# Reordered weight loads and a first token block in two halves, in a sketched-attention and squared-ReLU FFN kernel on one Trainium2 core

## Chip, cores and metric

The kernel runs on one NeuronCore of a Trainium2 chip. The metric is device time in microseconds (us), the median of several runs; lower is better. All else is read from one profiled execution of the kernel.

## What is computed

Polynomial-sketch linear attention over 4 batches, 4 heads, 1088 tokens and head size 32 is followed by a feed-forward block (FFN) with squared ReLU, from d_model 128 to d_ff 2048 and back. Everything is float32.

```python
def phi(x):                                   # x: [b, h, s, 32]
    a = np.einsum('rd,bhsd->bhsr', S1, x)     # r = 8
    b = np.einsum('rd,bhsd->bhsr', S2, x)
    return np.einsum('bhsi,bhsj->bhsij', a, b).reshape(*x.shape[:-1], 64)
q_p, k_p = phi(q), phi(k)
kv = np.einsum('bhsf,bhsd->bhfd', k_p, v)
z = np.sum(k_p, axis=2)
num = np.einsum('bhsf,bhfd->bhsd', q_p, kv)
den = np.einsum('bhsf,bhf->bhs', q_p, z)[..., None] + 1e-06
x = (num / den).transpose(0, 2, 1, 3).reshape(4352, 128)
h = np.maximum(x @ w_in, 0.0)
return h * h @ w_out
```

## The kernel before

The attention result is kept transposed in `xT` (128 features by 4352 tokens). The FFN walks over ten token chunks (`FC`: 256, 384, 448, 448, then five of 512 and a last one of 256). For a chunk, d_ff is cut into 16 blocks of 128. A *unit* is a group of blocks that fills one PSUM tile of 512 columns: in the first chunk two units of one block and seven of two blocks. Each unit goes through four steps:

- `ffn1` (L600): first matmul, `pg <- xT, w_in`, in the one-pass type fp32r. One record of the trace per block.
- `relu` (L610 on VectorE, L612 on ScalarE): `gt <- pg`.
- `square` (L623 on ScalarE, L625 on VectorE): `g <- gt`.
- `ffn2` (L644; L639 for the last chunk): second matmul, `po <- g, w_o`, in fp32, summed over the 16 blocks in PSUM. Two records per block.

`pg` has two PSUM buffers, so the first matmul of a unit waits for the relu two units back.

The first 256 tokens of batch 0 have a path of their own, written out by hand before line 854: `kf` (L318) sketches the keys with weights 64 or 32 columns wide, `kvp` (L399) sums keys against values, and `dT`, `rd`, `bc` and `xT` (L847 to L854, all on VectorE) form the reciprocal of the denominator, spread it and multiply. Between them `a_rep_kv` (L449, ScalarE) copies kv, and one matmul on `w_in` (L845, tile `warm`) is issued before the first FFN matmul. The rest of batch 0 comes in two further chunks of 384 and 448 tokens. Each takes these steps: transpose of q (`qT`, L299, VectorE), sketch of q (`qc`, L306, TensorE), reciprocals of the denominators (`rc`, L505), 16 small copies of them on GpSimd (`rd`, L513), shuffles and products (L522, L537), numerators (`nd`, L553, TensorE), the spread of the reciprocals (`bc`, L563) and the product into `xT` (L570). The first 384-wide FFN matmul needs that second chunk's `xT`.

Loads are issued on SyncE's queue in the order of the program, and each waits for the one eight places earlier to land: k, q's first 256 tokens and v of batch 0, q's next 384, the pieces of `w_in` (256 KB each, L208) and `w_o` (L217), q's last 448, and then batches 1 and 2. GpSimd casts each piece of `w_in` to fp32r (L688), ahead of its `rd` copies. Piece c of either weight serves blocks 4c to 4c+3.

```python
load_wi(nc.sync, 0)
load_wi(nc.sync, 1)
load_wi(nc.sync, 2)
load_wo(nc.sync, 0)
load_wo(nc.sync, 1)
load_wi(nc.sync, 3)
for c in range(2, 4):
    load_wo(nc.sync, c)
load_q(nc.sync, 0, 640, S)
```

From there on the order of instructions on each engine comes from a planner, `_Order`: operations with estimated times, needs and keys are placed greedily, engine by engine, and then emitted. TensorE's FFN order is fixed in advance by `seq`: the first matmuls of `LU = 4` units run ahead, and then each step emits the second matmuls of one unit (two units after the first chunk) and the first matmuls of units that come due. Batch 1's loads (`loads`) are such an operation. v of batch 1 has padding columns that GpSimd sets to zero, with a memset early in the program.

`f_last` closes the kernel: the last 256 tokens lie in `po[0]` and `po[1]`, ScalarE copies the first to SBUF (L682), VectorE the second (L684), and each is stored by two DMAs.

## Time and profile before

| | us |
|---|---|
| median of 3 runs | 185.08 |
| lowest and highest | 184.76, 185.16 |
| the profiled execution: its own time | 184.68 |
| its span from first to last instruction | 182.8 |
| TensorE busy | 177.8 (97%) |
| ScalarE busy | 136.5 (75%) |
| VectorE busy | 121.8 (67%) |
| GpSimd busy | 38.5 (21%) |

PE is TensorE's matmuls, PEld its weight loads, DVE VectorE, ACT ScalarE, POOL GpSimd, SP SyncE; a q behind the name is the engine's instruction queue, which waits or issues DMAs. A row of the timeline gives the start, the length and the engine of a merged group, its line, operation, tiles (written <- read) and shapes, the number of records, and in brackets the engine's idle time just before it with what ended it. Ends of matmuls are modelled, so successive matmuls may overlap in the rows; starts are the safer reading. A slice of the page is 4.57 us, a digit the share in tenths.

### The profile page before, as it was taken

The page shows a single profiled execution, that of the slowest core. Times are in us where ns is not written, and L with a number is a line of the kernel's source. Part 1 is how long each engine was busy: PE and PEld are TensorE (multiplying, and loading weights), DVE is VectorE, ACT ScalarE, POOL GpSimd, SP SyncE. Part 2 cuts the span into 40 slices and gives each one's busy share as a digit, 9 for nine tenths or more (in the row PEclk, how much of TensorE's full clock was granted, in tenths as well). Part 3 has the DMA queues.
Part 4 walks back from the last instruction along what each step waited for, and adds up shares of the span by engine and source line. Part 5 has one row for each costly group of instructions (what it writes and reads, how often), then busy time and mean ns, then how long its engine had stood idle before and what let it go on. Part 6 is the DMA issues. An engine that isn't in the chain of part 4 may idle for free.

```text
span 182.8 us, 3998 instructions
## 1 busy us (share of the span) xinstructions
PE 177.8 (97%) x1530; PEld 104.8 (57%) x1530; DVE 121.8 (67%) x262; ACT 136.5 (75%) x259; POOL 38.5 (21%) x158
## 2 busy tenths in 40 slices
PE   8999899999999999999999999999999999999992
PEld 2868676655645655555455554545555555555792
DVE  5979679999999962799994335996353334333640
ACT  3449479849948886799937778894777777777990
POOL 3545208438300002570008100500000000000000
PEclk9999999999999999999999999999999999999999
DMA  5799994010029700000030200003003000300111
GB/s 172 194 285 305 234 251 132 4 32 0 0 39 243 181 0 4 4 2 0 0 54 14 43 0 5 0 0 59 0 4 57 0 0 5 52 0 0 33 28 29
DMA packets 26147, 11.26 MB, mean 62 GB/s; under 512 B 17937, under 2 KB 25105, under 8 KB 26129
## 3 DMA queue, kind: packets, MB, share of 16 engines
q1 hardware_dynamic: 25936, 10.95, 24.9%
q8 instruction: 12, 0.20, 0.5%
q10 hardware_dynamic: 192, 0.07, 0.1%
q14 instruction: 7, 0.05, 0.1%
HBM read 8.78 MB, written 2.23 MB: 60 GB/s over the span
## 4 chain that ended last, share of the span: by engine, by line
PE 86%; SPq 6%; DMA 4%; DVE 1%; issue 1%
PE po L644 58%; PE pg L600 17%; DMA qn<-in_q_dram 4%; PE nd L553 3%; PE po L639 2%; PE pol L639 2%; SPq L217 2%; SPq L199 2%; SPq L208 1%; PE qc L306 1%; PE nd L417 1%; PE qc L350 1%; PE kvp L417 1%; SPq L187 0%; SPq L181 0%
## 5 line engine op out<-in xcount | busy, mean ns | idle before, releaser
L644 PE MATMUL po<-g,w_o 128*128 128x512 f32 (+3 forms) x288 | 122.7, 547 | 0.1
L612 ACT ACTIVATE gt<-pg 128x512 f32<-128x512 f32 (+3 forms) x144 | 75.2, 570 | 32.1 <-PE pg L600 31.5
L644 PEld LDWEIGHTS po<-g,w_o 128*128 128x128 f32 x288 | 53.4, 189 | 32.1 <-issue 24.4
L600 PE MATMUL pg<-xT,w_in 128*128 128x512 f32 (+3 forms) x160 | 70.1, 519 | 0.5 <-DVE xT L570 0.5
L623 ACT ACTIVATE g<-gt 128x512 f32<-128x512 f32 (+2 forms) x102 | 60.7, 623 | 1.6
L625 DVE TENSOR_TENSOR g<-gt 128x512 f32<-128x512 f32 (+3 forms) x43 | 30.0, 699 | 39.5 <-ACT gt L612 38.8
L600 PEld LDWEIGHTS pg<-xT,w_in 128*128 128x128 f32 x160 | 29.2, 190 | 29.2 <-ACT gt L612 11.5
L513 POOL COPY rd<-rc 32x9 f32<-32x9 f32 (+2 forms) x80 | 19.1, 239 | 27.0 <-DVE rc L505 23.8
L459 POOL COPY kv<-kvt 32x64 f32<-32x64 f32 x48 | 12.7, 264 | 44.7 <-DVE kvt L436 42.5
L522 DVE STREAM_SHUFFLE qa<-qc 128x576 f32<-128x576 f32 (+2 forms) x20 | 11.8, 652 | 0.0
L537 DVE TENSOR_TENSOR qp<-qa,qb 128x576 f32<-128x576 f32 (+2 forms) x20 | 10.8, 605 | 0.0
L485 DVE STREAM_TRANSPOSE qt<-qc 128x576 f32<-128x576 f32 (+2 forms) x10 | 5.8, 610 | 5.7 <-PE qc L350 4.0
L370 DVE TENSOR_TENSOR kp<-fs 128x576 f32<-128x576 f32 x12 | 8.8, 747 | 0.0
L648 DVE STREAM_TRANSPOSE oT<-po 128x512 f32<-128x512 f32 (+3 forms) x9 | 5.9, 654 | 2.1 <-PE po L644 2.1
L299 DVE STREAM_TRANSPOSE qT<-qn 128x192 f32<-128x192 f32 (+3 forms) x11 | 5.8, 560 | 1.7 <-DMA qn<-in_q_dram 1.7
L553 PE MATMUL nd<-qp,kv 32*32 32x288 f32 (+2 forms) x320 | 6.6, 354 | 0.0
L522 DVE STREAM_SHUFFLE qb<-qc 128x576 f32<-128x576 f32 (+2 forms) x10 | 6.1, 650 | 0.0
L570 DVE TENSOR_TENSOR xT<-nd,bc 128x576 fp32r<-128x576 f32 (+2 forms) x10 | 5.6, 594 | 0.5 <-PE nd L553 0.5
L639 PE MATMUL po<-w_o,g 128*128 128x128 f32 x32 | 5.8, 279 | 0.0
L639 PE MATMUL pol<-w_o,g 128*128 128x128 f32 x32 | 5.7, 275 | 0.0
L563 DVE STREAM_TRANSPOSE bc<-rd 128x576 f32<-128x576 f32 (+2 forms) x10 | 5.7, 598 | 0.0
L553 PEld LDWEIGHTS nd<-qp,kv 32*32 32x32 f32 x320 | 2.9, 103 | 3.6 <-issue 2.4
(106 smaller groups left out, 90.0 us busy)
## 6 DMA issues: line engine op xcount, KB each, us to landing
kn<-in_k_dram SPq DMA_DIRECT2D x3, 544.0 KB, 8.3
qn<-in_q_dram SPq DMA_DIRECT2D x3, 544.0 KB, 9.8
vn<-in_v_dram SPq DMA_DIRECT2D x9, 144.0 KB, 6.6
w_in<-in_moe_w_in_dram SPq DMA_DIRECT2D x4, 256.0 KB, 4.3
w_o<-in_moe_w_out_dram SPq DMA_DIRECT2D x4, 256.0 KB, 5.2
out_dram<-oT SPq DMA_DIRECT2D x12, 64.0 KB, 1.9
out_dram<-oT SPq DMA_DIRECT2D x8, 56.0 KB, 1.8
out_dram<-oT SPq DMA_DIRECT2D x8, 48.0 KB, 1.8
```

Source lines behind the costliest of these rows:

```text
L370: nc.vector.tensor_tensor(out=_ap(st[b, "kp"], 0, 128, 64 * NT * h, [[64, NT], [8, 8], [1, 8]]), in0=_ap(fs, 0, 128, o, [[32, NT], [1, 8], ...
L459: nc.gpsimd.tensor_copy(_ap(st[b, "kv"], 32 * c, 32, 64 * h, [[32, E], [1, 32]]), _ap(st["kvt"], 32 * h, 32, 0, [[64, E], [1, 32]]),)
L513: nc.gpsimd.tensor_copy(st[b, "rd", i0][32 * h : 32 * h + 32, n * c : n * c + n], st["rc"][32 * c : 32 * c + 32, n * h : n * h + n],)
L522: nc.vector.stream_shuffle(in_=banks(st[b, "qc", i0], 2 * x, 0, m), out=_ap(st[b, which, i0], 0, 128, 2 * m * x, [[m, 2], [1, m]]), mask=m ...
L537: nc.vector.tensor_tensor(out=st[b, "qp", i0, e][:, r], in0=st[b, f"qa{e}", i0][:, r], in1=st[b, "qb", i0][:, r], op=mult,)
L553: nc.tensor.matmul(nd[32 * h : 32 * h + 32, 512 * c : 512 * c + m], kv[r, o : o + 32], qp[r, m * h : m * h + m], start=(e == 0), stop=(e = ...
L600: nc.tensor.matmul(st["pg", u][:, n * i : n * i + n], w_in[:, 128 * (d0 + i) : 128 * (d0 + i) + 128], xT[:, c0 : c0 + n],)
L612: nc.scalar.activation(gt[:, 0:w], st["pg", u][:, 0:w], Relu)
L623: nc.scalar.activation(to, of, Square)
L625: nc.vector.tensor_tensor(out=to, in0=of, in1=of, op=mult)
L639: nc.tensor.matmul(po[x // 128][:, 0:128], g[:, x : x + 128], w, start=(d == 0), stop=(d == NB - 1),)
L644: nc.tensor.matmul(po[0][:, 0:n], w, g, start=(d == 0), stop=(d == NB - 1))
```

## The change

- The weight pieces alternate: w_in 0, w_o 0, w_in 1, w_o 1, w_in 2, w_o 2, w_in 3, then q's last 448 tokens, then w_o 3.
- The zeros of batch 1's v are written by GpSimd behind the second chunk's `rd` copies, and the zeroed range takes in the last column of a v row. v of batch 1 (its fourth part first) and q of batch 1 are issued behind that memset. For later batches v's parts are reversed too.
- The spread `bc0` and the product into `xT` of the first 256 tokens come in two halves of 128. Between them the first matmul and the relu of block 0 for the first half are emitted, and then the copy of kv; the square of that half is emitted behind, ahead of the next transpose of q.
- Block 0 of the first chunk is now two units of 128 tokens each, followed by block 1 alone and seven units of two blocks. The relu on VectorE is now that of block 1 (unit 2).
- `LU` becomes 3 for the first two steps of `seq` and 4 behind them.
- The matmul on `w_in` at L845 goes; the two key-sketch tiles with 64-wide weights become 32-wide.
- In `f_last` the second copy is cut: VectorE copies 64 columns and ScalarE the other 64.

```diff
-    LU = 4
+    LU = 3, 4
...
-            sizes = [1, 1] + [2] * 7
+            sizes = [1] + [2] * 7
+            d0 = 1
+            units += [(0, c0, 128, 0, 1)] * 2
+            dur += [5 * 128 / 2400 + 0.015] * 2
...
-            xT[:, c0 : c0 + n],
+            xT[:, c0 + part.get(u, 0) : c0 + part.get(u, 0) + n],
...
-            nc.tensor.matmul(po[0][:, 0:n], w, g, start=(d == 0), stop=(d == NB - 1))
+            x = part.get(u, 0)
+            nc.tensor.matmul(
+                po[0][:, x : x + n], w, g, start=(d == 0 and x == 0), stop=(d == NB - 1),
+                skip_group_check=(ci == 0),
+            )
...
-        nc.vector.tensor_copy(ob[1][:, :], po[1][:, 0:128])
+        nc.vector.tensor_copy(ob[1][:, 0:64], po[1][:, 0:64])
+        nc.scalar.copy(ob[1][:, 64:128], po[1][:, 64:128])
...
-    load_wi(nc.sync, 0)
-    load_wi(nc.sync, 1)
-    load_wi(nc.sync, 2)
-    load_wo(nc.sync, 0)
-    load_wo(nc.sync, 1)
-    load_wi(nc.sync, 3)
-    for c in range(2, 4):
+    for c in range(4):
+        load_wi(nc.sync, c)
+        if c == 3:
+            load_q(nc.sync, 0, 640, S)
         load_wo(nc.sync, c)
-    load_q(nc.sync, 0, 640, S)
...
-    nc.gpsimd.memset(_ap(vn[1], 96, 32, 32 * (NT - 2), [[32 * NT, H], [1, 64]]), 0.0)
...
-    a_kf(7, 2, psf, "pg", 64)
+    a_kf(7, 2, psf, "pg")
...
-    a_rep_kv(x0, 256)
-    st["warm"] = psf.tile([128, 512], F32, tag="po", name="warm")
-    for _ in range(W3):
-        nc.tensor.matmul(st["warm"][:, :], w_in[:, 0:128], w_in[:, 0:512])
...
-    bc0 = wpool.tile([128, 256], F32, tag="bc0", bufs=1, name="bc0")
-    nc.vector.transpose(bc0[:, :], _ap(rd0, 0, 128, 0, [[1, 8], [0, 32]]))
-    nc.vector.tensor_tensor(
-        out=xT[:, 0:256], in0=num0[:, 0:256], in1=bc0[:, :], op=mult
-    )
+    for x in range(2):
+        bc0 = wpool.tile([128, 128], F32, tag="bc0", bufs=2, name="bc0")
+        r = slice(128 * x, 128 * x + 128)
+        nc.vector.transpose(bc0[:, :], _ap(rd0, 0, 128, 4 * x, [[1, 4], [0, 32]]))
+        nc.vector.tensor_tensor(out=xT[:, r], in0=num0[:, r], in1=bc0[:, :], op=mult)
+        if x == 0:
+            ffn1(0, 0)
+            relu(0, "ACT")
+            a_rep_kv(x0, 256)
+    square(0, "DVE")
     a_qT(0, 14, 6)
...
+    def pad_v(b):
+        nc.gpsimd.memset(_ap(vn[b], 96, 32, 32 * (NT - 2) - 1, [[32 * NT, H], [1, 65]]), 0.0)
...
+        if b == 1:
+            i0 = AC[0][1][0]
+            O.add(
+                ("pad", b), {"POOL": 0.4}, s0, [("rl", 0, i0, c) for c in range(4)], on(pad_v, b),
+            )
+            O.add(("ldv", b), {"SP": 1.0}, s0, [("pad", b), ("ld", b)], on(loads_vq, b))
...
-    seq = [x for u in range(LU) for x in pe1[u]]
+    seq = [x for u in range(LU[0]) for x in pe1[u]]
+    ahead = LU[0]
...
-        held += range(u + LU, min(u + LU + g, NU))
+        to = min(u + g + LU[u > 1], NU)
+        held += range(ahead, to)
+        ahead = to
```

More of the change, by code (lines that the diff above doesn't have):

```diff
@@ L128 @@
     GT, G2, LA = 4, 6, 3.5
-    LU = 4
+    LU = 3, 4
     KC = [(0, 160), (160, 128)]
-    W0, W1, W3 = 8, 0, 1
+    W0, W1 = 8, 0
     ND, QT, WI, KL, QL = 2, 6.0, (1.0, 1.9), (30.0, 8.0), 4.0
@@ L310, in sketch, with a_kf @@
                 )
-    def a_kf(t0, n, pool, tag, w=32):
+    def a_kf(t0, n, pool, tag):
         kf = pool.tile([128, 512], F32, tag=tag, name="kf")
         for t in range(n):
-            for c in range(0, 128, w):
+            for c in range(0, 128, 32):
                 o = 128 * (t0 + t) + c
                 nc.tensor.matmul(
-                    _ap(kf, c, w, 32 * t, [[32 * n, 2], [1, 32]]),
-                    kt0[:, o : o + w],
+                    _ap(kf, c, 32, 32 * t, [[32 * n, 2], [1, 32]]),
+                    kt0[:, o : o + 32],
                     sf,
@@ L578 @@
     units, first_unit, dur = [], {}, []
+    part = {0: 0, 1: 128}
     for ci, (c0, n) in enumerate(FC):
@@ L582 @@
         sizes = [nb] * (NB // nb)
+        d0 = 0
         if ci == 0:
-            sizes = [1, 1] + [2] * 7
-        d0 = 0
+            sizes = [1] + [2] * 7
+            d0 = 1
+            units += [(0, c0, 128, 0, 1)] * 2
+            dur += [5 * 128 / 2400 + 0.015] * 2
         for m in sizes:
@@ L630, in ffn2 @@
         d = d0 + i
-        if d == 0:
+        if d == 0 and u != 1:
             st["po", c0] = [psf.tile([128, 512], F32, tag="po", name="po")]
@@ L986, in loads, with loads_vq @@
         load_k(nc.sync, b)
-        for p in range(4):
+        if b > 1:
+            loads_vq(b)
+    def loads_vq(b):
+        for p in range(3, -1, -1):
             load_v(nc.sync, b, p)
         load_q(nc.sync, b, 0, S)
+    def pad_v(b):
+        nc.gpsimd.memset(_ap(vn[b], 96, 32, 32 * (NT - 2) - 1, [[32 * NT, H], [1, 65]]), 0.0)
     prev["qTuse"] = []
@@ L1000, in k_load @@
         )
+        if b == 1:
[4 more added lines that the diff above has]
+            O.add(("ldv", b), {"SP": 1.0}, s0, [("pad", b), ("ld", b)], on(loads_vq, b))
         for x, y, t in (("ld", "kn", 6.0), ("kn", "vn", 3.0), ("vn", "qn", 3.0)):
-            O.add((y, b), {"IO": t}, s0, [(x, b)], lambda eng: None)
+            O.add(
+                (y, b), {"IO": t}, s0, [(x, b)] + ([("ldv", b)] if y == "vn" else []), lambda eng: None
+            )
         for i0, n in ((0, 18), (18, 16)):
@@ L1088 @@
             O.add(
-                mm1s[i], {"PE": n / 2400 + 0.01},
-                tu[u] - LA + 0.001 * i, xt, on(ffn1, u, i),
+                mm1s[i], {"PE": n / 2400 + 0.01 if u else 0.0},
+                tu[u] - LA + 0.001 * i, xt, on(ffn1, u, i) if u else lambda eng: None,
                 rings=[("pg" if u else "po", 2)] if i == 0 else [], lag=0.05,
@@ L1093 @@
         O.add(
-            ("relu", u), {"DVE": dve(w) + 0.06} if u == 1 else {"ACT": act(w)},
-            tu[u] - (1.2 if u != 1 else 41.0), [], lambda eng, u=u: relu(u, eng), uses=mm1s,
+            ("relu", u), {"DVE": dve(w) + 0.06} if u == 2 else {"ACT": act(w) if u else 0.0},
+            tu[u] - (1.2 if u != 2 else 41.0), [], lambda eng, u=u: relu(u, eng) if u else None,
+            uses=mm1s,
             rings=[("gt", GT)],
@@ L1099 @@
             ("sq", u),
-            {"DVE": dve(w)} if u < ND else
+            {"DVE": dve(w) if u else 0.0} if u < ND else
             {"ACT": 0.095 + w / 1200, "DVE": dve(w)},
             tu[u] - (0.6 if u > 1 else 40.0), [],
-            lambda eng, u=u: square(u, eng), uses=[("relu", u)], rings=[("g2", G2)],
+            lambda eng, u=u: square(u, eng) if u else None, uses=[("relu", u)], rings=[("g2", G2)],
             late={"DVE": 0.0, "ACT": 0.2 if u > 1 else 0.0},
@@ L1113 @@
                 on(ffn2, u, mm[2], xs[j // m]), uses=[("sq", u)],
-                rings=[("po", 2)] if d0 + j == 0 else [], lag=0.05,
+                rings=[("po", 2)] if d0 + j == 0 and u != 1 else [], lag=0.05,
             )
```

## The prediction, made before the changed kernel was run

> **What bounds the kernel now.** I read the page first, its slices and its chain, then the timeline from 12 to 24 us, the waits of that stretch, and the timeline of the last five microseconds.

> ```profile
> PE 177.8 (97%) x1530; PEld 104.8 (57%) x1530; DVE 121.8 (67%) x262; ACT 136.5 (75%) x259; POOL 38.5 (21%) x158
> PE   8999899999999999999999999999999999999992
> DMA  5799994010029700000030200003003000300111
> PE 86%; SPq 6%; DMA 4%; DVE 1%; issue 1%
> ```

> TensorE sets the time. From 24 us to the last matmul the chain is PE alone: a pair of 384-wide blocks costs 1.64 us again and again (chain: 27.65, 29.29, 30.93, 32.57). So only three stretches can pay: the start (first FFN matmul at 12.19), the stalls between 12 and 22.3, and what follows the last matmul. Whatever TensorE gains or loses by 22.3 us is carried to the end unchanged.

> ```profile
> 12.19 0.68 PE L600 MATMUL pg<-xT,w_in 128*128 128x256 f32 x4
> 13.24 0.47 PE L600 MATMUL pg<-xT,w_in 128*128 128x256 f32 x2
> 13.78 0.67 PE L644 MATMUL po<-g,w_o 128*128 128x256 f32 x2
> 15.19 1.03 PE L644 MATMUL po<-g,w_o 128*128 128x256 f32 x4
> 16.29 1.03 PE L644 MATMUL po<-g,w_o 128*128 128x256 f32 x4
> 18.58 0.96 PE L553 MATMUL nd<-qp,kv 32*32 32x96 f32 x64
> 19.47 1.99 PE L644 MATMUL po<-g,w_o 128*128 128x256 f32 x8
> 22.02 0.41 PE L600 MATMUL pg<-xT,w_in 128*128 128x384 f32 x1 [0.55 <-DVE xT L570]
> 22.27 1.02 PE L644 MATMUL po<-g,w_o 128*128 128x256 f32 x4
> ```

> Two records are one fp32 matmul, so x4 is two d_ff blocks. From 15.19 TensorE repeats every 1.10 us (two second matmuls, 0.865, and a pair of first matmuls, 0.235) and is full. The eight records at 19.47 start 0.216 us apart (the second after 0.32), so their work ends at 21.30, not at the row's modelled end; then TensorE stands 0.7 us for xT.

> ```profile
> 14.06 1.26 ACT L612 ACTIVATE gt<-pg 128x512 f32<-128x512 f32 x2
> 15.22 1.14 ACT L623 ACTIVATE g<-gt 128x512 f32<-128x512 f32 x2
> 16.26 1.08 ACT L612 ACTIVATE gt<-pg 128x512 f32<-128x512 f32 x2
> 15.19 0.61 POOL L688 CAST w_in<-w_in 128x512 fp32r<-128x512 f32 x1 [2.16 <-DMA w_in<-in_moe_w_in_dram]
> 15.75 3.83 POOL L513 COPY rd<-rc 32x3 f32<-32x3 f32 x16
> 19.65 0.70 DVE L299 STREAM_TRANSPOSE qT<-qn 128x256 f32<-128x256 f32 x2 [1.37 <-DMA qn<-in_q_dram]
> 21.51 0.36 DVE L570 TENSOR_TENSOR xT<-nd,bc 128x192 fp32r<-128x192 f32 x1
> ```

> Why xT is late: VectorE waits 1.37 us for q's last part (issued 12.99, landed 19.62), and the square, the denominators and xT queue behind. ScalarE runs gapless, about 0.5 us a step: two relus and two squares for four blocks take 2.0 us, against TensorE's 2.2. It has almost no slack either.

> ```profile
> 178.69 0.27 ACT L682 COPY obl<-po 128x128 f32<-128x128 f32 x1 [0.80 <-PE po L639]
> 179.58 0.29 DVE L684 COPY obl<-pol 128x128 f32<-128x128 f32 x1 [2.21 <-PE pol L639]
> ```

> After the last matmul come one 0.29 us copy and two stores, to 182.8.

> **Part 1, the start in halves.** Before: broadcast 11.10 (0.45), multiply 11.64 to 12.06, first matmul 12.19. A VectorE step loses about 0.13 us from 256 to 128 columns (256 wide 0.42, 192 wide 0.35). So the first half's xT runs 11.50 to 11.80, its matmul at 11.92: 0.27 earlier. The second half comes later: broadcast 11.7, multiply 12.1 to 12.4, matmul 12.53, then block 1 whole at 12.6.

> What follows is pushed back. On VectorE the square of half one now stands ahead of the transpose of q (before at 11.99): ScalarE's relu 12.2 to 12.5, square 12.55, transpose 12.75 to 13.1. TensorE's sketch of q (L306, before 12.79) needs it and runs to 13.6, where before it was through at 13.2. And blocks 2 and 3, before multiplied ahead of that sketch at 12.47 (part of the x4), now stand behind it and behind the first half's second matmul (0.22): 13.85 to 14.1. ScalarE's first 512-wide relu, which ran at 12.90, starts at 14.25.

> From there ScalarE sets the pace, by the steps of the rows: relu 14.25, relu 14.75, square 15.25 to 15.9, square, relu 16.27 to 16.86. TensorE can start the second matmuls of blocks 2 and 3 at 16.0 instead of 15.19 and its next pair of first matmuls at 17.0; that pair is done at 17.25. Before, the same work was done at 16.29: a lag of 0.95 us (0.7 with all hops at their shortest, 1.2 if each stall also shows a weight load of 0.07 us).

> **Part 2, weights and q.** Of the pieces only places in SP's queue change. By place: w_in's second piece takes the old third place (its cast waited until 12.42 before), the third the old fifth (issued 9.48, plus about 5: 14.5), the fourth the old seventh (10.79 + 5.2 = 16.0, before 15.14). The casts then end at 13.0, 15.1 and 16.7; TensorE wants them at 14.3, 15.5 and 18.1, so none delays it. The second matmul's wait for w_o's first piece (13.65 before) goes, but TensorE gets there at 13.6 anyway: nothing gained. q's last part goes out at 11.48 instead of 12.99 and by its 6.63 us lands near 18.1 to 18.6. VectorE reaches it after the first denominators at about 18.9: the 1.37 us wait goes.

> What is late next is GpSimd. Its 16 copies of reciprocals stand behind the fourth cast and start at 16.7 instead of 15.75; with their 3.83 us they end at 20.5. Second denominators 20.6 to 20.95, the two multiplies to 21.6: xT is there 0.25 us sooner than before (21.87).

> **Part 3, where both meet.** From the pair done at 16.29 TensorE needed 5.01 us without a stall to 21.30; the same work now runs 17.25 to 22.26, after xT. So the 0.7 us stall is gone and the lag has taken its place. The next second matmul follows 0.17 us behind (22.43, against 22.27): +0.16. With the lag's ends, -0.1 to +0.4; I take +0.2, nearer the end with reloads because every stall in these rows shows them. A shorter lag would find xT in its way: at 21.6 it allows -0.4 and no more.

> **Part 4, the end.** The last copy is cut: VectorE does 64 columns, ScalarE the other 64. In the built order ScalarE's half waits on VectorE, not on TensorE, so they run in a row. VectorE 0.29 - 0.07 = 0.22 (0.07 for 64 columns as above), a hop of about 0.06 and ScalarE 0.27 - 0.05 = 0.22: 0.50 instead of 0.29, **+0.21** on both stores. Ends +0.1 and +0.3; -0.07 if the halves did run together.

> **At nothing.** The 64-wide key matmuls become 32-wide: four more matmuls in a row of 64 records that takes 1.37, at most 0.17 us; the kvp matmuls wait for VectorE's kp to 8.6, which covers it. The warm-up matmul (0.50) ran while TensorE waited for xT. The pad memset (0.31 at 6.74) left GpSimd 2.63 us idle before the first cast; now it comes at 20.5, with 7.4 us of idle before GpSimd's next work. SP holds v of batch 1, then q of batch 1 and batch 2's loads, until 20.9 instead of 14.2. v needs up to 9 us and is wanted at 35.2 (L417), q of batch 1 at 36.7, k of batch 2 at 39.6: 3 to 5 us of cover, lost one for one beyond that. w_o's last piece lands one place later, near 19.6, wanted at 22.4.

> **Sum.** 0.20 + 0.21 = +0.41 us. The profiled execution took 184.68 (span 182.8 and 1.9 around it): 185.1. Against the median of the runs, 185.08, the forecast is 185.5. A measurement here tells about 0.2%, 0.37 us, from no change, so the forecast lies just over that line.

> **The rivals.**
> A, the sum: 185.5, own range 185.2 to 185.8; chance 0.62, of which 0.37 slower by over 0.2% and 0.25 within.
> B, faster: ScalarE's stream is not late. If blocks 2 and 3 start their second matmul by about 15.3, there is no lag, and with xT early the 0.7 us stall is a plain gain: 185.08 - 0.7 + 0.21 = 184.6. For it: the first matmul does come 0.27 earlier. Against: half of the block's first relus moves behind the sketch. It decides at a lag under 0.2, with xT by 21.4. Chance 0.12.
> C, later xT: GpSimd's copies end after 21.3, so that TensorE waits again. One copy among the products at 16.83 took 0.376 against 0.18. If all 16 stretched by 0.1 and the cast came 0.3 late, xT ends at 23.5 and it costs 1.2 more: 186.7; halfway, 186.0. It decides when the copies end after 21.1. Chance 0.18. [...]
> D, the cut copies do run side by side: -0.07 in place of +0.21, 185.2. Against: the wait stands in the order. Chance 0.05.
> E, the clock: PEclk is 9 in every slice before, yet the eight warm-ups up to 4.3 us stood 0.43 us apart, about twice the 0.23 of later 512-column matmuls (chain: pg L600 x2 in 0.46). If the thinner stretch at 12 to 13.6 let the clock fall again for 3.4 us of work, it costs 1.7: 187.2. Chance 0.03. [...]

> Slower 0.37 + 0.18 + 0.03 = 0.58; within 0.25 + 0.05 = 0.30; faster 0.12. The range takes in A and D whole, half of C and the near edge of B: 184.7 to 186.2.

> **What would show it.** Right: first pg near 11.9; the row of second matmuls of blocks 2 and 3 near 16.0; no wait of qT for qn; the 384-wide pg with no idle before it, at 22.2 or 22.3; an ACT copy into obl after the DVE one, stores at 180.1 plus the shift. Wrong: a po row of four records by 15.3 (B), idle before the 384-wide pg (C), both obl copies at one time (D), PEclk under 9 (E), or a PE stall after 24 us that names vn or qn.

## The result, and the profile after

The changed kernel takes 186.25 us (median of 22 runs, 185.73 to 188.02) against 184.71 (22 runs, 183.95 to 186.76) for the kernel before, measured side by side: ratio 1.0088, 95% interval 1.0072 to 1.0104. That is 1.5 us slower where 0.4 was forecast. The profiled execution took 186.98, span 185.16.

From the page of the changed kernel: busy time, slices, and the chain's shares.

```profile
PE 179.2 (97%) x1540; PEld 106.3 (57%) x1540; DVE 122.2 (66%) x264; ACT 137.3 (74%) x262; POOL 39.2 (21%) x158
PE   7989999999999999999999999999999999999992
PEclk9996999999999999999999999999999999999999
PE 93%; DMA 3%; DVE 1%; issue 1%; SPq 0%; ACT 0%; ACTq 0%
```

TensorE is still the engine that sets the time, but slice four has a 6 in the clock row where before all were 9. The windows (columns: length; busy us and instructions of PE, PEld, DVE, ACT, POOL; granted clock; DMA share; GB/s) put edges on it.

```profile
10.52:13.93 3.41, 2.68 (x59) 1.43 (x53) 2.78 (x10) 0.95 (x5) 1.22 (x2) 1.00 0.88 254
13.93:17.35 3.42, 3.42 (x34) 3.17 (x14) 3.10 (x18) 2.16 (x5) 1.15 (x2) 0.50 1.08 331
```

Half clock from 13.93 to 17.35: rival E, in this execution. The timeline of the same stretch:

```profile
12.14 0.30 PE L604 MATMUL pg<-xT,w_in 128*128 128x128 f32 x1
...
13.62 0.45 PE L306 MATMUL qc<-qT,sw 32*32 32x96 f32 x28 [0.20 <-DVE qT L299]
...
17.49 1.02 PE L649 MATMUL po<-g,w_o 128*128 128x256 f32 x4
...
23.52 0.53 PE L604 MATMUL pg<-xT,w_in 128*128 128x384 f32 x1
12.78 0.50 DVE L629 TENSOR_TENSOR g<-gt 128x128 f32<-128x128 f32 x1 [0.25 <-ACT gt L616]
12.52 0.61 POOL L697 CAST w_in<-w_in 128x512 fp32r<-128x512 f32 x1 [1.32 <-DMA w_in<-in_moe_w_in_dram]
17.37 4.38 POOL L513 COPY rd<-rc 32x3 f32<-32x3 f32 x16
```

The row of four is the second matmuls of blocks 2 and 3 (before 15.19), and the first 384-wide first matmul (`pg`) comes at 23.52 (before 22.02), with no idle ahead of it. That is +1.50 in all. A second loss was in no step of the prediction. It lies in a run of short matmuls at 36 to 39 us (`nd`, then keys against values at L417, then `nd` again):

```profile
38.11 0.49 PE L553 MATMUL nd<-qp,kv 32*32 32x128 f32 x29
38.96 0.40 PE L553 MATMUL nd<-qp,kv 32*32 32x128 f32 x3 [0.37 <-issue]
39.30 0.91 PE L649 MATMUL po<-g,w_o 128*128 128x384 f32 x2
```

In the kernel before the same 32 came in one row and the next po 0.43 us behind its start:

```profile
36.49 0.50 PE L553 MATMUL nd<-qp,kv 32*32 32x128 f32 x32
36.92 0.91 PE L644 MATMUL po<-g,w_o 128*128 128x384 f32 x2
```

TensorE stops after 29 records, released by "issue": nothing that the profile shows. The whole burst, from the first `nd` to that po, took 2.89 us against 2.13 before. From the first 384-wide to the first 448-wide pg it is 18.95 against 18.12, +0.83. After that nothing differs by more than 0.2 until the tail:

```profile
181.78 0.23 DVE L692 COPY obl<-pol 128x64 f32<-128x64 f32 x1 [2.20 <-PE pol L643]
182.04 0.21 ACT L693 COPY obl<-pol 128x64 f32<-128x64 f32 x1 [0.89 <-DVE obl L692]
```

The two copies run in a row. From the start of the last matmul to the last store it is 0.81 us, before 0.63: +0.18. Of that 0.11 reaches the end of the span, which comes 3.69 us after that matmul, before 3.58.

### The profile page after: what moved, and what is told of

It reads as the page before. It is cut to its first block, busy times and chain, and to the rows that moved or that the text cites. A ratio compares the mean times of both kernels' runs of the same rounds, so it can differ in the third digit from the quotient of the medians.

```text
span 185.2 us, 4024 instructions
## 1 busy us (share of the span) xinstructions
PE 179.2 (97%) x1540; PEld 106.3 (57%) x1540; DVE 122.2 (66%) x264; ACT 137.3 (74%) x262; POOL 39.2 (21%) x158
## 4 chain that ended last, share of the span: by engine, by line
PE 93%; DMA 3%; DVE 1%; issue 1%; SPq 0%; ACT 0%; ACTq 0%
PE po L649 60%; PE pg L604 18%; PE nd L553 3%; DMA qn<-in_q_dram 2%; PE po L643 2%; PE pol L643 2%; PE qc L306 2%; DMA vn<-in_v_dram 1%; PE nd L417 1%; PE qc L350 1%; PE kvp L399 1%; PE kvp L417 1%; SPq L181 0%; PE nd L350 0%; PE den L829 0%
## 5 line engine op out<-in xcount | busy, mean ns | idle before, releaser
L649 PE MATMUL po<-g,w_o 128*128 128x512 f32 (+4 forms) x290 | 124.0, 548 | 0.0
L649 PEld LDWEIGHTS po<-g,w_o 128*128 128x128 f32 x290 | 54.4, 192 | 31.8 <-issue 24.9
L604 PE MATMUL pg<-xT,w_in 128*128 128x512 f32 (+4 forms) x161 | 71.5, 525 | 0.2 <-DVE xT L856 0.2
L627 ACT ACTIVATE g<-gt 128x512 f32<-128x512 f32 (+3 forms) x103 | 61.1, 621 | 2.3 <-DVE gt L614 0.7
L604 PEld LDWEIGHTS pg<-xT,w_in 128*128 128x128 f32 x161 | 30.1, 197 | 28.8 <-ACT gt L616 12.0
L513 POOL COPY rd<-rc 32x9 f32<-32x9 f32 (+2 forms) x80 | 19.6, 246 | 26.2 <-DVE rc L505 23.0
L553 PE MATMUL nd<-qp,kv 32*32 32x288 f32 (+2 forms) x320 | 7.0, 354 | 0.4 <-issue 0.4
L299 DVE STREAM_TRANSPOSE qT<-qn 128x192 f32<-128x192 f32 (+3 forms) x11 | 5.8, 554 | 0.4 <-DMA qn<-in_q_dram 0.4
L570 DVE TENSOR_TENSOR xT<-nd,bc 128x576 fp32r<-128x576 f32 (+2 forms) x10 | 5.5, 587 | 0.5 <-PE nd L553 0.5
L553 PEld LDWEIGHTS nd<-qp,kv 32*32 32x32 f32 x320 | 3.0, 103 | 4.4 <-issue 3.1
```

Of the source, the lines that this page charges most:

```text
L513: nc.gpsimd.tensor_copy(st[b, "rd", i0][32 * h : 32 * h + 32, n * c : n * c + n], st["rc"][32 * c : 32 * c + 32, n * h : n * h + n],)
L553: nc.tensor.matmul(nd[32 * h : 32 * h + 32, 512 * c : 512 * c + m], kv[r, o : o + 32], qp[r, m * h : m * h + m], start=(e == 0), stop=(e = ...
L604: nc.tensor.matmul(st["pg", u][:, n * i : n * i + n], w_in[:, 128 * (d0 + i) : 128 * (d0 + i) + 128], xT[:, c0 + part.get(u, 0) : c0 + par ...
L627: nc.scalar.activation(to, of, Square)
L649: nc.tensor.matmul(po[0][:, x : x + n], w, g, start=(d == 0 and x == 0), stop=(d == NB - 1), skip_group_check=(ci == 0),)
```

## The experiments

Times are medians beside runs of the kernel before on the same chip; the ratio and its interval stand behind. L is the lag of the start, S the stop in the burst, K the half clock.

| run | what it is | this / before, us | ratio, 95% |
|---|---|---|---|
| e1 | before + loads and late pad | 185.31 / 184.15 | 1.0065 [1.0033, 1.0097] |
| e2 | before + halves, no warm-up, 32-wide key sketches | 186.06 / 184.15 | 1.0087 [1.0057, 1.0117] |
| e3 | changed + warm-up | 186.05 / 184.15 | 1.0096 [1.0065, 1.0127] |
| e4 | before + cut tail | 184.67 / 184.15 | 1.0019 [0.9996, 1.0041] |
| e5 | changed, 64-wide | 186.21 / 184.52 | 1.0093 [1.0070, 1.0117] |
| e6 | before, 32-wide | 184.88 / 184.52 | 1.0035 [1.0002, 1.0068] |
| e7 | before + weights' and q's order | 184.63 / 184.52 | 1.0008 [0.9984, 1.0031] |
| e8 | before + late pad | 184.30 / 184.52 | 0.9995 [0.9981, 1.0010] |
| f1 | changed, again | 186.57 / 184.11 | 1.0132 [1.0116, 1.0148] |
| f2 | changed, 64-wide + warm-up | 185.48 / 184.11 | 1.0074 [1.0060, 1.0088] |
| f3 | changed, four units ahead | 185.76 / 184.11 | 1.0092 [1.0078, 1.0106] |
| f4 | f3, 64-wide, old tail | 185.74 / 184.11 | 1.0085 [1.0073, 1.0098] |
| g1 | before, again | 184.33 / 184.49 | 0.9992 [0.9973, 1.0012] |
| g2 | halves alone, 64-wide, warm-up | 185.90 / 184.49 | 1.0059 [1.0036, 1.0082] |
| g3 | before without warm-up | 184.43 / 184.49 | 0.9999 [0.9971, 1.0026] |

### Which part carries it: e1, e2, e4, e3

e1 and e4 take one part of the diff alone, e2 the halves together with the two small edits to TensorE's matmuls (no warm-up, 32-wide key sketches), and e3 the whole with the warm-up put back.

> The kernel before with the order of loads and the late zeros of v alone. Theory clock (the half clock from 13.9 to 17.4 us cost about 1 us, and comes from the thin start of the halves): no half clock here. Theory GpSimd (the fourth cast and the 16 copies of rd end later, at 21.7 instead of 19.6): xT near 22.6, the first 384-wide matmul 0.3 to 0.6 us later than 22.0, total +0.3 to +0.6. The prediction's own sum without a lag: xT at 21.6, total -0.3.

> The changed kernel with the load order, the zeros of v and the last copy as before: halves, unit split, LU 3,4, no warm-up on w_in. Theory clock: the thin stretch from 11.9 to 13.9 is still there, so a half clock follows for 3.4 us and the total is 1.0 to 1.4 over before. Theory lag (the order of steps on ScalarE alone): at most +0.3, as xT waits for q as before and hides the lag.

> The kernel before with the last copy cut between VectorE and ScalarE. The prediction: +0.21 us (0.1 to 0.3), ScalarE's copy starting after VectorE's ends. Rival: both run together, -0.07.

```diff
e4, on the kernel before
-        nc.vector.tensor_copy(ob[1][:, :], po[1][:, 0:128])
+        nc.vector.tensor_copy(ob[1][:, 0:64], po[1][:, 0:64])
+        nc.scalar.copy(ob[1][:, 64:128], po[1][:, 64:128])
```

The halves with those two edits (e2) cost as much as the whole change; one run of six had half clock, and the median of the five others is 185.99. The tail took 0.35 us more by the ratio, with zero inside the interval; the trace has the same +0.18 at the last store and +0.11 at the end. The loads were slower too, with a wide spread: seven runs from 184.6 to 185.7, three from 186.4 to 186.7, all at full clock. The profile of e1 is of one of the fastest (184.69) and shows no loss.

> The changed kernel with the one matmul on w_in put back ahead of the first FFN matmul. Theory clock: TensorE's window from 10.5 to 13.9 is fuller by one 512-column matmul; if that holds the clock, 0.6 to 1.2 less than the changed kernel (185.1 to 185.7); if one matmul is too little, the half clock stays and so does the time. Theory lag or fetch: no change, 186.2.

```diff
e3, on the changed kernel
+    st["warm"] = psf.tile([128, 512], F32, tag="po", name="warm")
+    for _ in range(W3):
+        nc.tensor.matmul(st["warm"][:, :], w_in[:, 0:128], w_in[:, 0:512])
```

With the warm-up no run showed the half clock (mean clock 0.996 to 1.000), and the time was that of e2 all the same. So the clock alone does not carry the median.

### The stop in the burst: e5, e6

In every profile that shows TensorE's stop it stands at one place: behind record 1216. A record is one instruction of TensorE's stream in the trace, counted from 0, with weight loads, matmuls, the instructions that wait for semaphores and one drain at the start taken together (by loads and matmuls alone the place would vary by two). The 32-wide key matmuls are 16 such records more (four fp32 matmuls, each two passes of a load and a matmul); the block cut in two, less the warm-up and two waits, adds two. So the burst ends at record 1221 where it ended at 1203, and covers 1216.

> The changed kernel with the two key-sketch tiles multiplied in 64-wide pieces again: four fp32 matmuls (16 records of TensorE's stream, a weight load and a matmul for each of two passes) fewer near 7 us; all else as changed. Theory 1, a place in the instruction stream: TensorE stops for 0.48 to 0.64 us at its record 1216 whatever that record is; in the changed kernel this lies in the burst of short matmuls at 38 us, with 16 records fewer the burst ends at record 1206 and the stop falls among 0.32 us matmuls that hide it. Then from the burst's first nd to the next po takes 2.13 us (changed kernel 2.89), the stretch from the first 384-wide to the first 448-wide pg 18.1 to 18.3 (changed 18.95), and the time falls by 0.6 to 0.8 to about 185.4. Theory 2, the lag of the start alone: the burst stays at 2.8 to 2.9 and the time within 0.2 of the changed kernel's 186.1. Theory 3, the clock: half clock in some runs; the time of the others does not move.

> The kernel before with one edit of the change alone: the two key-sketch tiles in 32-wide pieces, so that TensorE's stream is 16 records longer from about 7 us on. Theory 1, a place in the instruction stream: the burst of short matmuls ends at record 1220 and covers record 1216, so the stop of about 0.5 to 0.6 us shows in it; burst 2.6 to 2.9 us in place of 2.13, the time 0.5 to 0.7 over before. The prediction's step (at most 0.17, covered) and theory 2: burst 2.13, the time within 0.2 of before.

```diff
e6, on the kernel before (e5 does the reverse on the changed kernel)
-    a_kf(7, 2, psf, "pg", 64)
+    a_kf(7, 2, psf, "pg")
```

e6's timeline: one edit at 7 us, and the stop is in the burst 29 us later, with nothing else of the change there.

```profile
35.92 0.49 PE L553 MATMUL nd<-qp,kv 32*32 32x128 f32 x30
37.25 0.37 PE L553 MATMUL nd<-qp,kv 32*32 32x128 f32 x2 [0.84 <-issue]
37.56 0.91 PE L644 MATMUL po<-g,w_o 128*128 128x384 f32 x2
```

The burst took 3.34 us (record 1216 to 1217: 1.10), and in e5 2.14. The place is shown in both directions. The price is not: e6 is 0.36 slower by medians (0.65 by the ratio, interval 0.04 to 1.25), but e5 did not get faster than the changed kernel, against theory 1. e5's profile has half clock from 14.79 to 18.21, and its first 384-wide pg is at 23.89.

What goes with the stop: on the queue that the profile calls "q8 instruction" one 16 KB packet goes out before each of these places. In all seven profiles that show the stop, TensorE goes on 1.2 to 1.5 us after that packet ends (changed kernel 37.59, then 38.96; f1 36.63, then 38.12; e6 35.76, then 37.25). In the ten without it, record 1217 comes 1.4 us or more after the packet's end anyway. Each profile has twelve such packets, against 3099 to 3122 records of TensorE's stream: about 260 records to a packet, if the packets carry that stream (an estimate from the two counts). In the kernel before, where the place falls among matmuls 0.32 us apart, nothing of a stop is seen: record 1217 comes 0.32 us behind 1216, at 38.66. In the changed kernel it falls into the burst, 289 records in 2.1 us, and the same step takes 0.63 us, from 38.33 to 38.96. That TensorE waits there for what the packet brings (the "fetch" of e3's expectation) is argued from these times; no run moved the packets themselves.

### The loads one by one: e7, e8

> The kernel before with the new places in SP's queue alone (weights in turn, q's last part ahead of w_o's last), without the late pad zeros and the late v of batch 1. The loads together took 1.0065 [1.0033, 1.0097] of before. If the order is what costs, by the later fourth cast and GpSimd's copies behind it or by k and v of batch 0 coming late, this shows 1.004 to 1.009. If the late v costs, this is within 0.2% of before or faster by up to 0.3 us, since q's last part no longer holds VectorE (the wait of 1.37 us on qn gone) and the first 384-wide pg comes 9.1 us after the first pg (before 9.83).

> The kernel before with the late pad zeros alone: batch 1's v, then its q, issued behind GpSimd's copies near 20 us, the weights' order as before. If the late v costs, the time is 0.5 to 1.2 us over before and a stall of TensorE after 24 us names vn, qn or kn; if the order costs, within 0.2% of before and no such stall. The prediction's step (3 to 5 us of cover): within 0.2%.

```diff
e7, on the kernel before
-    load_wi(nc.sync, 0)
...
-    load_q(nc.sync, 0, 640, S)
+    for c in range(4):
+        load_wi(nc.sync, c)
+        if c == 3:
+            load_q(nc.sync, 0, 640, S)
+        load_wo(nc.sync, c)
```

e8 takes the pad and the late v of batch 1 from the diff in the same way. Neither costs anything that can be told. In e7's timeline the wait for q is gone and two others have its place: TensorE waits for a cast of `w_in`, of which the prediction said that none delays it, and VectorE waits for GpSimd's copies, which start at 17.02. So the first 384-wide pg came 10.13 us after the first pg, and not 9.1 as expected.

```profile
15.57 0.50 PE L600 MATMUL pg<-xT,w_in 128*128 128x256 f32 x2 [0.54 <-POOL w_in L688]
19.11 0.38 DVE L563 STREAM_TRANSPOSE bc<-rd 128x192 f32<-128x192 f32 x1 [0.96 <-POOL rd L513]
21.39 0.38 DVE L563 STREAM_TRANSPOSE bc<-rd 128x192 f32<-128x192 f32 x1 [0.48 <-POOL rd L513]
```

Why both together (e1) took 0.65% more is not settled; behind the halves they add nothing that can be told (f2 against g2 below).

### The changed kernel again, and with causes taken out: f1 to f4

> The changed kernel unaltered, as the yardstick for the runs beside it, and for its variation. Time 1.007 to 1.011 of before. Theory L (the lag of the start carries it; the kernel before only had a late q in its profile, most executions have no stall before the first 384-wide pg): whatever the clock, the second matmuls of d_ff blocks 2 and 3 start over 4.0 us after the first pg, the first 384-wide pg over 10.0 us after it (the kernel before 3.0 and, without a late q, 8.9). Theory K (half clock in all runs of this kernel): the window of half clock is there again and in most runs the mean clock is 0.991.

> The changed kernel with two things put back: the key sketches in 64-wide pieces (no stop of TensorE in the burst at 38 us) and the warm-up matmul (no half clock in the profile of the run that had it). Theory S (the stop at record 1216 costs the timed runs what it costs the profile): 0.6 to 0.8 us under the changed kernel beside it. Rival: the stop is smaller without the profiler, within 0.3 of the changed kernel. In both, burst of 2.13 us in the profile and no half clock.

> The changed kernel with four units of first matmuls issued ahead in place of three: those of d_ff blocks 2 and 3 stand directly behind the sketch of q again and no longer behind the second matmul of the first half block. Theory L (the lag is ScalarE's late start on 512-wide relus, so TensorE's second matmuls of blocks 2 and 3 come late): the first 512-wide relu comes 0.5 to 0.9 us earlier against the first pg (changed kernel 3.1 us after it), and the time falls by 0.4 to 0.9. Rival (the lag is work of TensorE and VectorE, not the order): within 0.2 of the changed kernel.

> The changed kernel with what theories L and S and the tail name put right at once: four units ahead, 64-wide key sketches, the last copy whole. What is left of the change is the start in halves, the loads and the late pad. If L, S and the tail (0.2) add up: 1.2 to 1.8 us under the changed kernel, 184.3 to 184.9, within 0.2% of before. If a cause is missing: 0.5 us or more over before.

```diff
f2 is e5 and e3 together; f3, on the changed kernel (f4 adds e5's edit and takes back e4's)
-    LU = 3, 4
+    LU = 4, 4
```

f1's profile fell on an execution at full clock. Its timeline:

```profile
11.99 0.30 PE L604 MATMUL pg<-xT,w_in 128*128 128x128 f32 x1
...
13.64 0.49 PE L649 MATMUL po<-g,w_o 128*128 128x128 f32 x2
...
16.09 1.13 PE L649 MATMUL po<-g,w_o 128*128 128x256 f32 x4
...
22.27 0.53 PE L604 MATMUL pg<-xT,w_in 128*128 128x384 f32 x1
...
38.12 0.40 PE L553 MATMUL nd<-qp,kv 32*32 32x128 f32 x3 [0.79 <-issue]
```

That is the prediction's start, point for point, and the run took 186.08, 2.0 us over the median of the kernel before beside it, all the same. Of four runs three had a mean clock of 0.991 (186.46 to 186.94), one of 1.000 (186.08).

f2, with the stop and the half clock out (burst 2.13 us, clock 0.996 or over in all five runs), is 1.1 us under f1, and 0.6 under f1's run at full clock. Theory S expected 0.6 to 0.8. It is still 1.4 us over before.

f3 is a miss of theory L's detail: the first 512-wide relu came 2.19 us after the first pg, in f1 2.42, not 0.5 to 0.9 earlier; the 384-wide pg came 10.06 after it against 10.28. Its 0.3 us under f1's run at full clock are about what a shorter start (0.2) gives. f4 missed its sum: 185.74, not 184.3 to 184.9. In its profile TensorE waits 0.21 us for xT ahead of the first 384-wide pg (22.72), the stop is there again, ten records behind the burst (0.77 us where 0.32 is usual; that time the packet ended at 38.28), and two of its five runs had a clock of 0.991. So the order ahead does not remove the lag; what is left as its cause is the halving itself.

### The kernel before again, the halves alone, and the warm-up: g1, g2, g3

> The kernel before, unaltered, for a second profile of it. Theory L (the 0.7 us stall of TensorE before the first 384-wide pg, against which the prediction set the lag, belongs to the one execution shown, whose q came late): no idle before that matmul, which comes 8.8 to 9.2 us after the first pg (first profile 9.83), and VectorE waits under 0.5 us for qn (first profile 1.37). Rival (the stall is the kernel's own): 0.5 us of idle or more, 9.7 to 9.9 us. Time within 0.2% of before in both.

> The start in halves alone: weights, pad and last copy as before, key sketches 64-wide, warm-up matmul kept. Theory L: with the stop of TensorE's stream, the half clock and the tail all out, only the lag is left; the first 384-wide pg comes 10.0 to 10.4 us after the first pg, and the time is 0.7 to 1.1 us over before. The prediction's part 1 with part 3 (lag against a stall that is there anyway): 0.1 to 0.4 over before. Theory X (a cause that is still not seen): over 1.3.

> The kernel before without the one warm-up matmul that the change removes too (L845, 0.50 us while TensorE waits for xT). Theory K (without it, TensorE's stretch near 12 us is thin enough for the clock to fall): half clock for 3.4 us in some executions (mean clock 0.991), and those 0.5 to 1.7 us longer. Rival (the halves make the stretch thin, not the missing warm-up): no run under 0.996, time within 0.2% of before. If either: the first pg comes up to 0.2 earlier.

```diff
g2, on e2: a_kf as in e5, the warm-up as in e3; g3, on the kernel before
-    st["warm"] = psf.tile([128, 512], F32, tag="po", name="warm")
-    for _ in range(W3):
-        nc.tensor.matmul(st["warm"][:, :], w_in[:, 0:128], w_in[:, 0:512])
```

g1, the second profile of the unaltered kernel:

```profile
14.44 0.67 PE L644 MATMUL po<-g,w_o 128*128 128x256 f32 x2 [0.67 <-DMA w_o<-in_moe_w_out_dram]
...
22.31 0.41 PE L600 MATMUL pg<-xT,w_in 128*128 128x384 f32 x1 [0.19 <-DVE xT L570]
```

And e4, whose start is that of the kernel before:

```profile
21.63 0.52 PE L600 MATMUL pg<-xT,w_in 128*128 128x384 f32 x1
```

Neither theory had this right. The idle ahead of the 384-wide pg is 0.19, not 0.55, but another load, w_o's first piece, held TensorE 0.67 us at 14.44. Six profiles have the start of the kernel before (before, e4, e6, e8, g1, and g3 but for the warm-up). Their first 384-wide pg comes at 22.02, 21.63, 21.14, 21.69, 22.31 and 21.35, mean 21.69; in e4, e6, e8 and g3 TensorE waits for xT not at all. So the stall that the prediction leaned on belongs to two executions of six, in full to one. These two are the only profiles of the unaltered kernel itself. But g1's fell on one of its slower runs, 184.95 where the median is 184.33, and from that matmul to the end of the span both profiles take the same 160.8 us; so the median run of g1 would have it about 0.6 us earlier than 22.31, near 21.7 (an estimate from these numbers). In f1 to f4, at full clock, the same matmul is at 22.27, 22.62, 22.39 and 22.72, mean 22.50: **+0.8 us**. Counted from the first pg, it is 9.3 and 10.3 on the mean.

g2 times the lag with nothing else: 1.0059 [1.0036, 1.0082], 1.1 us by the ratio, the upper end of theory L; by the medians it is 1.4, beyond theory L and inside X. The interval, 0.7 to 1.5 us, leaves both open. Its own profile fell on an execution with half clock (14.32 to 17.73), so the place is read in f2 (22.62, with no idle ahead of it).

g3 is as fast as before without the warm-up, yet two of its 12 runs had a clock of 0.991 (186.16 and 185.62; the ten others median 184.23). The half clock counted over all runs, by a mean clock of 0.991 or less: unaltered kernel before 1 of 96; changed kernel 6 of 26; the seven other kernels with halves 6 of 42, two of these in g2, which has the warm-up; e6 2 of 12. Put by the warm-up, that is 12 of 59 without it (halves 10 of 47, g3 2 of 12), and with it 2 of 21 with the halves and 3 of 154 with the whole block. Both theories are half right: without the warm-up it comes more often, the warm-up does not exclude it, and what the halves add to that is not told by so few runs.

## Why the prediction was wrong

The direction was right, and so were most times in it. At full clock (f1) the first pg was at 11.99 (predicted 11.92), TensorE past q's sketch at 13.64 (13.6), the first 512-wide relu at 14.41 (14.25), the second matmuls of blocks 2 and 3 at 16.09 (16.0), the first 384-wide pg at 22.27 (22.26). That f1 matches to 0.01 is luck, since the start moves from execution to execution; from the first pg to the 384-wide one the prediction has 10.34, and f1 to f4 have 10.06 to 10.62. The tail was +0.18 at the last store by the trace (+0.21), though only 0.11 reached the end. What failed:

**Part 3, the comparison.** "The 0.7 us stall is gone and the lag has taken its place" set a lag of 0.95 against a stall of one execution and left +0.16. Most of the profiles with the start of the kernel before do not have that stall, so nearly the whole lag counts: +0.8 in the profiles, +1.1 in the timed runs of the halves alone. This is the largest error. It came from setting the sum against one profile and against 185.08, the median of three runs; the larger samples taken later have the kernel before at 184.1 to 184.7.

**"At nothing", the 32-wide key matmuls.** Their own time is covered, as said: the weight loads of the `kvp` matmuls behind them wait 0.7 us for VectorE's `kp` in the changed kernel's profile. That 16 more records early move a fixed place of TensorE's stream into the burst, where a stop has nothing to hide behind, was not thought of. The profiles show 0.48 to 1.10 us for the stop; the timed runs give 0.4 to 0.65 (f2 against f1's run at full clock and against e3, and e6), with e5 against it. Its price in the timed runs stays open.

**Rival E at 0.03, and the warm-up at nothing.** The half clock came in 6 of 26 runs of the changed kernel, with a price of 0.6 to 0.9 us (186.98, 186.71 and 187.04 against a median of 186.1 of the other 19; the few such runs of other kernels scatter from 0.1 to over 2). In the four profiles that have it the first 384-wide pg comes 11.20 to 11.76 us after the first pg, about 1.1 later than in f1 to f4. The prediction's price of 1.7 was too high for this kernel, perhaps since TensorE waits for other engines in that stretch anyway (argued, not tried apart); its chance was far too low. In the changed kernel's profile TensorE was busy 2.68 of the 3.41 us ahead of the fall. The four profiles that show it have 2.43 to 2.82 there, and it begins 10.24 us after full clock was granted, three times 3.41, in each (3.69 and 13.93 in the changed kernel). The share does not decide it alone, since e3 had a window with 1.81 and kept full clock.

**Part 1, the hops.** In the first profile of the changed kernel the square of half one took 0.50 us in place of 0.29, with GpSimd's cast at 12.52 beside it, and q's sketch waited 0.20 for what queued behind. In f1 the cast came at 12.07, and the square took 0.29. The same is seen in five profiles (changed kernel, e2, e3, e5, f4): the square of a half that starts with 0.2 us or more of a cast left takes 0.36 to 0.57 us and ends 0.13 to 0.15 after the cast, where others take 0.26 to 0.29. Rival C looked for GpSimd's copies stretched beside VectorE's products; here it is VectorE's square that is stretched beside GpSimd's cast.

**Right:** q's last part landed at 17.93 and VectorE's wait for it was gone; GpSimd's copies became late (17.37 to 21.75 in the first profile, 16.77 to 21.09 in f1, predicted 16.7 to 20.5), and hid behind the lag. Rival C's mechanism is there: VectorE waits for the copies 0.96 and 0.74 us in the changed kernel's profile, 0.30 and 0.75 in f1, 0.96 and 0.48 in e7. Of that only 0.21 us (f4) and 0.12 (e7) come through to TensorE as idle ahead of the 384-wide pg. D did not happen. The late v of batch 1 was covered (e8).

By the timed runs the sum at full clock is 1.1 (lag, g2), 0.35 (tail, e4; 0.11 by the traces) and 0.4 to 0.65 (stop): 1.9 to 2.1. Measured at full clock are 1.4 (the 19 runs, 186.1 against 184.71) and 2.0 (f1's one run against 184.11). So the terms do not close to better than about half a microsecond, and e5 says that one of them is taken too high.

## What to carry to other kernels

Before a stall in a profile is set against a cost, look whether it is in other executions: a wait for a load near the start can be one draw and no property of the kernel (VectorE waited for q 1.37 us in one profile of the kernel before and 0.59 in the other). Where there is only one profile, the sum without that stall belongs in the range. Count instructions as well as time: where short matmuls run through hundreds of records in 2 us, an edit ahead of them can move a place where TensorE stops in or out (16 records more in e6: 3.34 us for the burst; 16 fewer in e5: 2.14). Cutting the first tile in two brought its first matmul 0.2 us forward here (11.99 in f1, 12.19 before) and doubled the hops behind it; the argument, not tried in other forms, is that it pays only if the engine that follows was waiting for that matmul.
